# Attention on one core: the products with the values in two portions of 256 queries, other step costs in the plan, and later due times for the sums' transfers

## The chip, the core and the metric

The kernel runs on one core of a Trainium2 chip. The core has a TensorE (PE in the profile; PEld are its weight loads), a VectorE (DVE), a ScalarE (ACT), a GpSimd (POOL), a SyncE that only issues transfers (SP), and 16 DMA engines. The metric is the device time of one execution in microseconds (us); the figure for a kernel is the median of several executions.

## What is computed

Two kinds of layer alternate, twice: multi-head attention and a state-space convolution (S4D), each with a layer norm ahead and a residual sum behind. 2048 positions, 640 channels, 32 heads of 20 channels.

```python
def _A_ref(x, wqkv, wo):                     # attention
    qkv = (x @ wqkv).reshape(B, S, 3, H, Dh) ...
    scores = jnp.einsum("bhqd,bhkd->bhqk", q, k) * (Dh ** -0.5)
    p = _softmax(scores, axis=-1)
    o = jnp.einsum("bhqk,bhkd->bhqd", p, v)
    return o.transpose(0, 2, 1, 3).reshape(B, S, D) @ wo

def _B_ref(u, log_A_real, A_imag, C_real, C_imag, log_dt, D_skip):   # S4D
    P = jnp.exp((A * dt[:, None])[:, :, None] * pos[None, None, :])
    K = 2.0 * jnp.einsum("dn,dnl->dl", C, P).real    # convolution kernel, from the parameters alone
    y = irfft(rfft(u_t, 2 * L) * rfft(K, 2 * L)) ...
    return y + u * D_skip

x = x + _A_ref(_layernorm(x), A_wqkv, A_wo)
x = x + _B_ref(_layernorm(x), ...)
x = x + _A_ref(_layernorm(x), A_wqkv, A_wo)
x = x + _B_ref(_layernorm(x), ...)
```

## The kernel before, in words

**Stages.** Attention 1, output projection, S4D 1, attention 2, output projection, S4D 2. In attention 1 the S4D convolution kernel `K` is also made (`kgen`), since it depends on parameters alone; its second user, S4D 2, finds it stored. The change touches the two attention stages.

**One attention stage** is a loop over 8 groups `g` of four heads, 4 blocks `qb` of 512 queries and 16 blocks `kt` of 128 keys: 32 blocks (`g`, `qb`) of 16 steps `kt`. One step `kt` has two **waves** `j`, one for each pair of heads. A wave is: eight matmuls of the scores (L775, into the PSUM tile `S`), then one exponential on ACT (L778, `pt<-S`, 128x1024). There are 1024 waves in a stage; this text numbers them from 0 in each stage, so block (`g`, `qb`) begins at wave 128g + 32qb. Of `S` there are two buffers: the scores of wave n+2 wait for the exponential of wave n. Behind the second wave of a step come the products with the values (L792, `values`): eight float32 matmuls of 64 rows by 32 columns by 512 queries, into the two accumulators `pa`. The trace shows each float32 matmul as two records.

**What fills PE between the scores.** `jobs` yields steps of the projections for the later heads: `qk` steps of eight fp16 matmuls (L560, 15 steps for 512 queries of one 128-column block, four blocks `b` of 128 columns in all; their norms L488 close a block) and portions of the values of a group pair (`vq`, L524: 15 matmuls of 128x160 for each of 16 key tiles). In attention 1 there are also the contractions of `kgen` (L314, `contract`: two steps of 16 float32 matmuls each). `slot` puts one such step between two groups of scores if it fits by the plan.

**The plan.** The program is written out once, in Python; `Plan` holds three clocks (`pe`, `act`, `dve`) that are moved on by a cost in us for each step (0.22 for the scores, 0.865 for the values, 0.215 for a `qk` step, 0.43 for a contraction step, 0.63 for a portion of `vq`, 0.92 for an exponential). The order of PE's matmuls is fixed by it (`chain`), and so is the order of DVE's work and of the transfers on the queues of POOL and SP (`Ordered`). ACT's instructions and POOL's arithmetic are not tied: the scheduler places them. `AHEAD` is a table (wave, us of jobs done): contractions are taken only when the jobs are ahead of it. `need(...)` forces the jobs that a coming group depends on: block `b` of the projections must be complete, with norms, at `kt` = 10 of the last block ahead of the group that reads it (waves 116, 372, 500 and 756).

**The end of a block.** Behind its last values DVE adds the two accumulators (`oc<-pa`, twice). Then, at due times behind that (in us of the plan): `sums` (0.2) writes the rows of the denominators to memory (`dn<-oc`), `load` (5.0) reads them back in another shape (`dr<-dn`), `invert` (10.0) takes the reciprocal on DVE, `back` (11.0) writes it (`dn<-dr`), `spread` (15.5) reads it to all rows (`db<-dn`). At the end of the next block `scale` multiplies (`oc<-oc,db`) and `store` writes the result (`ot<-oc`). All these transfers are on POOL's queue, which also carries `kgen`'s loads of 576 KB (`kpw<-wd`) and stores (`kd<-ko`), and the bounds for the softmax (`qm<-mr`).

**The end of the stage.** When `kgen` is done and all heads are projected, `end_jobs` loads the output weights and splits them on POOL (`woh`, `wol`); `out_split` loads the first slices of the attention's result (`otl<-ot`) and splits them on ACT (`oh<-otl`) ahead of the output projection.

Of the kernel before, what the change touches and what calls it, by code (L numbers as in the profile page):

```python
# [29 lines left out]
NA, NB = 32, 64  # L30
LV = [1.0, 2.0, 4.0, 8.0, 16.0, 32.0, 64.0, 128.0, 256.0, 512.0, 1024.0, 1536.0]
PB = 7
AHEAD = ((0, 0.0), (96, 22.0), (352, 47.0), (478, 72.0), (724, 125.0))
WS = 256.0
LG = 2
BOUND = 30.0
# [45 lines left out]
def mha_s4d_kernel(ctx, tc, x_in, wqkv, wo, lar, aim, cr, ci, ldt, dsk,  # L82
# [96 lines left out]
    def kgen():  # L179
# [124 lines left out]
        def contract(r, bs, sub, ko, a, b):  # L304

            ps = pst("M", [P, 512], F32, tag=f"m{r}", name=f"m{r}")[:, :DC // 4 * NB].rearrange("p (c b) -> p c b", b=NB)
            for c8 in range(DC // 4):
                if c8:
                    yield plan.pe + 0.7, 0.43, True, ()
                plan.on_pe(0.43)  # L310
                for n in range(4):
                    for j in range(4):
                        ch, dd = DC * (sub % 2) + 4 * c8 + j, 4 * c8 + j
                        chain(te.matmul(ps[32 * j:32 * j + 32, c8, :], a[n // 2][:, ch, :], b[n][:, dd, :],  # L314
                                        start=(n == 0), stop=(n == 3), tile_position=(0, 32 * j)))
# [75 lines left out]
    def attention(x, stats):  # L391
# [121 lines left out]
        def values_of(i, q, ps, w, n):  # L513

            sl = slice(i * P, i * P + P)
            k = 0
            if n == QW:
                plan.on_pe(0.63)
            for ct in range(NCT):
                for a_, m in ((xh, w[0]), (xh, w[1]), (xl, w[0])):  # L520
                    if k == 8 and n == QW:
                        yield 0.0, 0.63, True, ()
                        plan.on_pe(0.63)
                    chain(te.matmul(ps[:, :n], a_[:, ct, sl], m[:, ct, :], start=(k == 0), stop=(k == 14)))  # L524
# [12 lines left out]
        def jobs():  # L537
# [40 lines left out]
            def vq(q):  # L578
                make = stage(2 * D + q * QW, QW, "v")
                yield plan.pe + 5.0, 0.0, False, ()  # L580
                w = make()
                t0 = plan.dve
                for i in range(NI):
                    yield t0, 0.63, False, (i % 2,)
# [38 lines left out]
        def slot(until=None):  # L623
# [4 lines left out]
            if pend and part[0] is None and not begun and (head[0] is None or spent[0] >= ahead(len(ends) - 2)):  # L628
# [1 line left out]
                r = free.index(min(free))  # L630
                t = max(t + 0.15, free[r])
                if t <= plan.pe or until is None and head[0] is None:
                    part[:] = f(r, *args), (t, 0.43, True, ())
                    pend.pop(0)
            step = part[1] if part[0] else head[0]
            if step is None:
# [144 lines left out]
            ends.append(plan.act)  # L781
            return pt

        def values(qb, g, kt, pts, pa):

            V = Vt[g // 2 % 3]
            plan.on_pe(0.865)
            for r in range(2):
                rows = slice(64 * r, 64 * r + 64)
                for j in range(4):  # L790
                    h = 4 * (g % 2) + j
                    chain(te.matmul(pa[r][32 * j:32 * j + 32, :], V[rows, kt, VP * h:VP * h + 32],  # L792
                                    pts[j // 2][rows, 512 * (j % 2):512 * (j % 2) + 512],
                                    start=(kt == 0), stop=(kt == NI - 1), tile_position=(64 * r, 32 * j)))
            if kt == NI - 1:
# [37 lines left out]
                def store():  # L833
# [1 line left out]
                        h = 4 * g + j  # L835
                        ge.dma_start(ot[h * DH:(h + 1) * DH, 512 * qb:512 * qb + 512], oc[32 * j:32 * j + DH, :])
                later.extend((plan.dve + n, f) for n, f in (
                    (0.2, sums), (5.0, load), (10.0, invert), (11.0, back), (15.5, spread)))
                later.sort(key=lambda e: e[0])
                scaled.append(scale)  # L840

# [22 lines left out]

        def fill(j):

            if ready:
                t = max(ready[0][0] + 0.15, 0.0 if ready[0][3] else sums_[0])
                if t <= plan.pe + 0.1 or j and len(ready) > 2:
                    plan.on_pe(0.0, t)  # L870
                    values(*ready.pop(0)[1:])
            while slot(plan.act - 0.5):
                pass
            drain_later()
            weave()
# [4 lines left out]
        for g in range(H // 4):  # L880
            need((0, 1, 1, 2, 3, 3, 4, 4)[g], ("v", g // 2))
            for qb in range(4):
# [9 lines left out]
                for kt in range(NI):  # L892
                    kc, pts = P * (kt % 8), []
                    for j in range(2):
                        pts.append(scores(kop[j][kt // 8], kc, qop[j][qb % 2]))
                        if j:
                            ready.append((plan.act, qb, g, kt, pts, pa))
                        fill(j)
                    if kt == 2:
                        for j in range(2):  # L900
# [519 lines left out]
```

## Time and profile before

| what | us |
|---|---|
| median of 3 runs | 2776.24 (2775.16 to 2778.0) |
| the profiled execution | 2777.71 |
| its span in the trace | 2775.8 |
| attention 1, first to last exponential | 111.8 to 1146.2 |
| attention 2, first to last exponential | 1564.0 to 2545.4 |
| busy: PE / ACT / DVE / POOL | 2544.2 / 2352.1 / 1469.0 / 821.2 |
| mean granted clock of TensorE | 0.987 |

A row of the timeline is: start in us from the span's start, time in us, engine, line, operation, out<-in, shape, xcount, and in brackets the engine's idle time just before and what ended it. Rows of one operation that follow each other are merged. A busy PE is not a PE at its peak: the end of a matmul is modelled and includes the time that it takes to run through the array, so the distance from one group's start to the next group's start is the better measure of what PE can do. L74 is the helper that records DVE's work and the transfers; such rows are told apart by their tiles.

### The profile page before, as it was taken

The numbers are of one execution on the slowest core, as the hardware profiler recorded it, in microseconds if no ns is written. First come the engines' busy times: TensorE is split into PE (matmuls) and PEld (weight loads), VectorE is DVE, ScalarE is ACT, GpSimd is POOL, SyncE is SP. The second block draws the span as 40 slices with busy tenths as digits, with TensorE's granted clock in tenths as the row PEclk, the third lists the DMA queues.
The fourth block names the chain that finished last, engine by engine and source line by source line (L and its number), as shares of the span: only waits on it lengthen the run. The fifth ranks groups of instructions, "written<-read, shape, count | busy, mean of one in ns | idle before, by whom it ended". The sixth has DMA issues, their size and how long they took to land.

```text
span 2775.8 us, 117573 instructions
## 1 busy us (share of the span) xinstructions
PE 2544.2 (92%) x51968; PEld 1436.6 (52%) x51968; DVE 1469.0 (53%) x3292; ACT 2352.1 (85%) x2781; POOL 821.2 (30%) x1232
## 2 busy tenths in 40 slices
PE   7898989999999997899999998999999888878998
PEld 3453544444444442587796544544444333335988
DVE  8645778978887870366777333332222100002865
ACT  8797989999999998645665698999999999997464
POOL 1112222323223324300573022222322422222376
PEclk9999999999999999999999999999999999999999
DMA  6512232323222223354543112111211211112365
GB/s 230 162 43 68 54 77 52 85 59 78 56 68 55 57 84 96 100 202 179 198 150 92 34 49 66 54 52 51 55 50 38 69 27 38 39 40 71 106 194 159
DMA packets 179128, 238.65 MB, mean 86 GB/s; under 512 B 36144, under 2 KB 124208, under 8 KB 176816
## 3 DMA queue, kind: packets, MB, share of 16 engines
q1 hardware_dynamic: 143168, 184.44, 20.6%
q0 software_dynamic: 35440, 46.58, 7.8%
q8 instruction: 410, 6.72, 1.0%
q14 instruction: 110, 0.90, 0.1%
HBM read 154.87 MB, written 76.03 MB: 83 GB/s over the span
## 4 chain that ended last, share of the span: by engine, by line
ACT 46%; PE 28%; issue 11%; DVE 7%; DMA 6%; POOL 1%; SPq 0%; ACTq 0%; DVEq 0%; POOLq 0%
ACT pt L778 46%; PE pa L792 4%; PE S L775 3%; PE psv L1148 3%; PE po L1054 3%; PE psy L1158 2%; PE psx L1136 2%; PE psx L1113 2%; PE po L1048 1%; DMA kop<-ks 1%; PE m L314 1%; PE pv L524 1%; PE pst L1123 1%; PE m L560 1%; PE pq L681 1%
## 5 line engine op out<-in xcount | busy, mean ns | idle before, releaser
L778 ACT ACTIVATE pt<-S 128x1024 f32<-128x1024 f32 x2048 | 1930.9, 1041 | 71.8 <-PE S L775 57.2
L792 PE MATMUL pa<-pt,V 64*32 64x512 f32 x16384 | 1099.6, 594 | 0.6 <-DVE oc L74 0.6
L775 PE MATMUL S<-qop,kop 61*32 61x512 f16 x16384 | 869.4, 383 | 160.6 <-ACT pt L778 138.0
L775 PEld LDWEIGHTS <-kop 61*32 61x32 f16 x16384 | 369.9, 90 | 830.7 <-issue 726.1
L74 POOL DMA_DIRECT2D dn<-oc x256 | 125.2, 496 | 835.6 <-DVE oc L74 768.2
L792 PEld LDWEIGHTS pa<-pt,V 64*32 64x32 f32 x16384 | 308.9, 107 | 69.4 <-issue 8.3
L74 DVE COPY oc<-pa 128x512 f32<-128x512 f32 x64 | 44.2, 691 | 414.8 <-PE pa L792 414.7
L74 DVE TENSOR_SCALAR qc<-m 128x512 f32<-128x512 f32 x64 | 44.1, 689 | 289.2 <-PE m L560 289.2
L74 POOL DMA_DIRECT2D db<-dn x256 | 129.3, 511 | 139.7 <-DMA dn<-dr 137.0
L74 DVE TENSOR_TENSOR kb<-ktab 128x512 f32<-128x512 f32 x240 | 155.3, 684 | 1.5 <-PE m L314 1.5
L560 PE MATMUL m<-xh,wh 64*32 64x512 f16 x2560 | 139.1, 380 | 3.0 <-DVE qc L74 3.0
L560 PE MATMUL m<-xh,wl 64*32 64x512 f16 x2560 | 138.3, 378 | 0.7 <-issue 0.7
L560 PE MATMUL m<-xl,wh 64*32 64x512 f16 x2560 | 138.4, 378 | 0.0
L74 POOL DMA_DIRECT2D ot<-oc x256 | 130.7, 517 | 8.9 <-DVE oc L74 6.0
L314 PEld LDWEIGHTS m<-kb,ka 128*32 128x32 f32 x5120 | 79.8, 110 | 101.6 <-issue 64.5
L560 PEld LDWEIGHTS <-wh 64*32 64x32 f16 x5120 | 87.7, 94 | 75.4 <-issue 37.6
L1141 POOL TENSOR_TENSOR t<-t,kb 128x512 f32<-128x512 f32 x80 | 102.1, 1276 | 70.3 <-DVE t L74 69.4
L1125 ACT COPY xt<-pst 128x1024 f16<-128x1024 f16 x80 | 81.6, 1023 | 46.7 <-PE pst L1123 46.5
L314 PE MATMUL m<-kb,ka 128*32 128x64 f32 x5120 | 105.8, 224 | 11.4 <-DVE qc L74 11.4
L74 POOL DMA_DIRECT2D dn<-dr x64 | 35.7, 557 | 234.1 <-DVE dr L74 229.8
L1142 POOL TENSOR_TENSOR t<-t,t 128x512 f32<-128x512 f32 x78 | 99.3, 1273 | 7.3 <-DVE t L74 1.3
L970 POOL TENSOR_TENSOR ul<-u,uh 128x640 f16<-128x640 f32 x30 | 46.5, 1566 | 177.7 <-ACT uh L969 177.7
(273 smaller groups left out, 3770.4 us busy)
## 6 DMA issues: line engine op xcount, KB each, us to landing
ka<-kha SPq DMA_DIRECT2D x80, 256.0 KB
kb<-khb SPq DMA_DIRECT2D x80, 256.0 KB
db<-dn POOLq DMA_DIRECT2D x256, 64.0 KB, 2.8
kpw<-wd POOLq DMA_DIRECT2D x20, 576.0 KB, 7.7
qop<-qs SPq DMA_DIRECT2D x256, 40.0 KB
kop<-ks SPq DMA_DIRECT2D x128, 80.0 KB
ot<-oc POOLq DMA_DIRECT2D x256, 40.0 KB, 2.6
otl<-ot SPq DMA_DIRECT2D x32, 320.0 KB
```

The lines of the kernel that those rows point to most:

```text
L74: made = f(out, *a, **k)
L314: chain(te.matmul(ps[32 * j:32 * j + 32, c8, :], a[n // 2][:, ch, :], b[n][:, dd, :], start=(n == 0), stop=(n == 3), tile_position=(0, 32 ...
L560: chain(te.matmul(ps[r][32 * t:32 * t + 32, :], a_[rows, ct, 32 * t:32 * t + 32], m[rows, ct, sl], start=(k == 0), stop=(k == 14), tile_po ...
L775: chain(te.matmul(S[32 * t:32 * t + 32, 512 * r:512 * r + 512], kt_[rows, kc + 32 * t:kc + 32 * t + 32], qt[rows, :], start=True, stop=Tru ...
L778: se.activation(pt, S, AF.Exp, scale=SCALE)
L792: chain(te.matmul(pa[r][32 * j:32 * j + 32, :], V[rows, kt, VP * h:VP * h + 32], pts[j // 2][rows, 512 * (j % 2):512 * (j % 2) + 512], sta ...
L1054: te.matmul(pos[hf], oh[:, ct, :], m[:, ct, 320 * hf:320 * hf + 320], start=False, stop=(ct == NCT - 1 and m is wol))
L1113: te.matmul(ps[:, r, i, :], e1[:, e, s, r, :], m[:, s, bs], start=(n == 0), stop=(n == 2))
L1125: se.copy(xt, pt.rearrange("p k g c -> p k (g c)"))
L1141: ge.tensor_mul(t2, t2, kb)
L1142: (ge if g0 else ve).tensor_add(t1, t1, t2)
L1148: te.matmul(pv[:, g].rearrange("p r i c -> p (r i c)"), t1[:, g * P:g * P + P], fa, start=True, stop=True)
```

## The change

The products with the values are cut in two portions of 256 queries (`half`), each planned at 0.433. A portion is queued by itself, and `fill` puts it between two groups of scores only if it ends 0.5 before the exponential does, or if more than five portions are waiting. A contraction step is counted at 0.56 where it was 0.43. A portion of `vq` ends every five matmuls (0.4 each) where it ended at the eighth (0.63 each). `AHEAD` asks for less of the jobs at most waves. The due times of `load`, `invert`, `back` and `spread` move from 5.0, 10.0, 11.0 and 15.5 to 6.0, 14.0, 14.5 and 20.0.

```diff
-AHEAD = ((0, 0.0), (96, 22.0), (352, 47.0), (478, 72.0), (724, 125.0))
+AHEAD = ((0, 0.0), (84, 20.0), (340, 44.0), (466, 68.0), (730, 122.0))
...
-                    yield plan.pe + 0.7, 0.43, True, ()
-                plan.on_pe(0.43)
+                    yield plan.pe + 0.7, 0.56, True, ()
+                plan.on_pe(0.56)
...
-                    if k == 8 and n == QW:
-                        yield 0.0, 0.63, True, ()
-                        plan.on_pe(0.63)
+                    if k % 5 == 0 and k and n == QW:
+                        yield 0.0, 0.4, True, ()
+                        plan.on_pe(0.4)
...
-        def values(qb, g, kt, pts, pa):
+        def values(half, qb, g, kt, pts, pa):
...
-            plan.on_pe(0.865)
+            plan.on_pe(0.433)
...
-                    h = 4 * (g % 2) + j
-                    chain(te.matmul(pa[r][32 * j:32 * j + 32, :], V[rows, kt, VP * h:VP * h + 32],
-                                    pts[j // 2][rows, 512 * (j % 2):512 * (j % 2) + 512],
-                                    start=(kt == 0), stop=(kt == NI - 1), tile_position=(64 * r, 32 * j)))
+                    h, c0 = 4 * (g % 2) + j, 256 * half
+                    chain(te.matmul(pa[r][32 * j:32 * j + 32, c0:c0 + 256], V[rows, kt, VP * h:VP * h + 32],
+                                    pts[j // 2][rows, 512 * (j % 2) + c0:512 * (j % 2) + c0 + 256],
+                                    start=(kt == half == 0), stop=(half == 1 and kt == NI - 1), tile_position=(64 * r, 32 * j)))
...
-                    (0.2, sums), (5.0, load), (10.0, invert), (11.0, back), (15.5, spread)))
+                    (0.2, sums), (6.0, load), (14.0, invert), (14.5, back), (20.0, spread)))
...
-            if ready:
-                t = max(ready[0][0] + 0.15, 0.0 if ready[0][3] else sums_[0])
-                if t <= plan.pe + 0.1 or j and len(ready) > 2:
-                    plan.on_pe(0.0, t)
-                    values(*ready.pop(0)[1:])
+            def half(late):
+                if not ready:
+                    return False
+                t = max(ready[0][0] + 0.15, 0.0 if ready[0][4] else sums_[0])
+                if not late and (t > plan.pe + 0.1 or plan.pe + 0.433 > plan.act - 0.5):
+                    return False
+                plan.on_pe(0.0, t)
+                values(*ready.pop(0)[1:])
+                return True
+            while len(ready) > 5:
+                half(True)
+            while len(ready) > 2 and half(False):
+                pass
             while slot(plan.act - 0.5):
                 pass
+            while half(False):
+                pass
...
-                            ready.append((plan.act, qb, g, kt, pts, pa))
+                            ready.extend((plan.act, n, qb, g, kt, pts, pa) for n in range(2))
```

Three places where the order moves, as the built programs have it.

PE in attention 1 ahead of the scores of wave 758 (tiles: `S` scores, `pa` the values' accumulators, `m` the PSUM tile of a projection or contraction). Before:

```order
L775 LDWEIGHTS kop_104
L775 MATMUL S<-qop_108,kop_104 32x512
L792 MATMUL pa_21160<-pt,V_94 32x512 x4
L792 MATMUL pa_21161<-pt,V_94 32x512 x4
L775 LDWEIGHTS kop_102
L775 MATMUL S<-qop_106,kop_102 32x512
```

And of the change, at the same wave:

```order
L775 LDWEIGHTS kop_104
L775 MATMUL S<-qop_108,kop_104 32x512
L792 MATMUL pa_23682<-pt,V_94 32x256 x4
L792 MATMUL pa_23683<-pt,V_94 32x256 x4
L792 MATMUL pa_23682<-pt,V_94 32x256 x4
L792 MATMUL pa_23683<-pt,V_94 32x256 x4
L314 MATMUL m_24258<-kb_24032,ka_23867 32x64 x4
L314 MATMUL m_24258<-kb_24033,ka_23867 32x64 x4
L314 MATMUL m_24258<-kb_24034,ka_23868 32x64 x4
L314 MATMUL m_24258<-kb_24035,ka_23868 32x64 x4
L524 LDWEIGHTS xh
L524 MATMUL m_24336<-vh,xh 128x160
```

Between the same two groups of scores there now stand both portions of the values, a contraction step, the 15 matmuls of a whole key tile of `vq` (the first of them is the last row shown) and then the norms L488 of the last projected block, which stood ahead of wave 743 before.

POOL's queue around the end of block 6 (it ends at wave 224), before:

```order
L74 DMA dn<-oc 16x1x32 x4
L74 DMA ot<-oc 20x512 x4
L74 DMA kpw_166<-wd 128x36x32
L74 DMA dr<-dn 128x16
L74 DMA dn<-dr 128x16
L74 DMA db<-dn 32x512 x4
```

And of the change:

```order
L74 DMA dn<-oc 16x1x32 x4
L74 DMA ot<-oc 20x512 x4
L74 DMA dr<-dn 128x16
L74 DMA dn<-dr 128x16
L74 DMA db<-dn 32x512 x4
L74 DMA kd<-ko 128x8x64
L74 DMA kpw_165<-wd 128x36x32
```

The load of the sums (`dr<-dn`) stood behind a load of `kgen` and now stands ahead of it.

ACT near the end of attention 1, before:

```order
L530 ACTIVATE V_94<-pv 128x8x20
L778 ACT_TABLE_LOAD
L778 ACTIVATE pt<-S 128x1024 x970
L956 CAST oh<-otl 128x640 x2
L778 ACTIVATE pt<-S 128x1024 x54
L956 CAST oh<-otl 128x640
```

And of the change:

```order
L778 ACTIVATE pt<-S 128x1024 x980
L966 CAST oh<-otl 128x640
L778 ACTIVATE pt<-S 128x1024 x8
L966 CAST oh<-otl 128x640
L778 ACTIVATE pt<-S 128x1024 x36
L966 CAST oh<-otl 128x640
```

The first two splits of the attention's result moved from behind 970 exponentials to behind 980 and 988. In attention 2 they stay behind 970. The last contraction stands ahead of wave 961 where it stood ahead of wave 911, and `end_jobs` moves from wave 928 to wave 992.

More of the change, by code (lines that the diff above doesn't have):

```diff
@@ L517, in values_of @@
             if n == QW:
-                plan.on_pe(0.63)
+                plan.on_pe(0.4)
             for ct in range(NCT):
                 for a_, m in ((xh, w[0]), (xh, w[1]), (xl, w[0])):
-                    if k == 8 and n == QW:
-                        yield 0.0, 0.63, True, ()
-                        plan.on_pe(0.63)
+                    if k % 5 == 0 and k and n == QW:
+                        yield 0.0, 0.4, True, ()
+                        plan.on_pe(0.4)
                     chain(te.matmul(ps[:, :n], a_[:, ct, sl], m[:, ct, :], start=(k == 0), stop=(k == 14)))
@@ L583, in vq @@
                 for i in range(NI):
-                    yield t0, 0.63, False, (i % 2,)
+                    yield t0, 0.4, False, (i % 2,)
                     yield from values_of(i, q, pst("M", [P, 512], F32, tag=f"m{i % 2}", name=f"m{i % 2}"), w, QW)
@@ L632, in slot @@
                 if t <= plan.pe or until is None and head[0] is None:
-                    part[:] = f(r, *args), (t, 0.43, True, ())
+                    part[:] = f(r, *args), (t, 0.56, True, ())
                     pend.pop(0)
@@ L790, in values @@
                 for j in range(4):
-                    h = 4 * (g % 2) + j
-                    chain(te.matmul(pa[r][32 * j:32 * j + 32, :], V[rows, kt, VP * h:VP * h + 32],
-                                    pts[j // 2][rows, 512 * (j % 2):512 * (j % 2) + 512],
-                                    start=(kt == 0), stop=(kt == NI - 1), tile_position=(64 * r, 32 * j)))
-            if kt == NI - 1:
+                    h, c0 = 4 * (g % 2) + j, 256 * half
+                    chain(te.matmul(pa[r][32 * j:32 * j + 32, c0:c0 + 256], V[rows, kt, VP * h:VP * h + 32],
+                                    pts[j // 2][rows, 512 * (j % 2) + c0:512 * (j % 2) + c0 + 256],
+                                    start=(kt == half == 0), stop=(half == 1 and kt == NI - 1), tile_position=(64 * r, 32 * j)))
+            if half and kt == NI - 1:
                 blk = 4 * g + qb
```

## The prediction

> **What bounds the kernel now.** I read the page's list of groups first, then the exponentials in windows, then the timeline of PE and of DVE where ACT waits. The change touches the two attention stages alone; ahead of them and behind them the order of PE is the same but for a few rows.
>
> ```profile
> L778 ACT ACTIVATE pt<-S 128x1024 f32<-128x1024 f32 x2048 | 1930.9, 1041 | 71.8 <-PE S L775 57.2
> ...
> 111.80:1146.20 1034.40, 973.57 (x1024) 0.98 0.27 66
> 1564.00:2545.40 981.40, 957.28 (x1024) 0.99 0.17 47
> 2200.00:2450.00 250.00, 249.94 (x273) 1.00 0.13 35
> ```
>
> The last three rows are the exponentials alone: window, its length, busy time, count. From 2200 on PE has nothing but scores and values, and ACT never waits: 249.94 / 273 = 0.9155 us for a wave, 1.83 for a step of two. At that rate 1024 waves take 937.5, so attention 1 lies 96.9 us and attention 2 43.9 us above ACT's own time. This is all that the change can win. The page shows 71.8 of it as idle time of ACT; the rest is exponentials that start just late enough not to overlap the one ahead.
>
> The first part of it is PE itself, where a step holds too much:
>
> ```profile
> 700.91 0.41 PE L775 MATMUL S<-qop,kop 61*32 61x512 f16 x8
> 701.13 1.04 PE L792 MATMUL pa<-pt,V 64*32 64x512 f32 x16
> 702.00 0.40 PE L775 MATMUL S<-qop,kop 61*32 61x512 f16 x8
> 702.32 0.65 PE L314 MATMUL m<-kb,ka 128*32 128x64 f32 x32
> 702.91 0.41 PE L775 MATMUL S<-qop,kop 61*32 61x512 f16 x8
> ```
>
> From start to start: scores 0.22, values 0.87, scores up to the contraction 0.32 (0.10 of it is the entry into the other form), contraction 0.59. The step is 2.00, or 0.17 over ACT's 1.83, though the plan counts 0.22 + 0.865 + 0.22 + 0.43 = 1.74. Two more forms:
>
> ```profile
> 263.98 0.41 PE L775 MATMUL S<-qop,kop 61*32 61x512 f16 x8
> 264.20 0.41 PE L560 MATMUL m<-xl,wh 64*32 64x512 f16 x8
> ...
> 264.85 0.41 PE L775 MATMUL S<-qop,kop 61*32 61x512 f16 x8
> ```
>
> ```profile
> 704.00 0.40 PE L775 MATMUL S<-qop,kop 61*32 61x512 f16 x8
> 704.33 0.24 PE L524 MATMUL m<-vh,xh 128*128 128x160 f16 x1
> ...
> 704.82 0.23 PE L524 MATMUL m<-vl,xh 128*128 128x160 f16 x1
> 704.99 0.41 PE L775 MATMUL S<-qop,kop 61*32 61x512 f16 x8
> ```
>
> A wave with three `qk` steps (each 0.22; the order has three between these two rows of scores) takes 0.87 (with the values' wave 1.96, 0.13 over). One with eight matmuls of `vq` takes 0.99 (2.08, 0.25 over): 0.22, eight times 0.07, and 0.21 for the entry; seven of them make 0.18 over, ten would make 0.39.
>
> The second part is waits of DVE that reach ACT:
>
> ```profile
> 261.38 1.87 POOL L74 DMA_DIRECT2D kpw<-wd  x1
> ...
> 263.25 0.56 POOL L74 DMA_DIRECT2D dr<-dn  x1
> ...
> 267.66 0.51 PE L775 MATMUL S<-qop,kop 61*32 61x512 f16 x8
> 268.95 0.17 DVE L74 TENSOR_SCALAR dr<-dr 128x16 f32<-128x16 f32 x1 [4.57 <-DMA dr<-dn]
> ...
> 271.81 0.84 PE L314 MATMUL m<-kb,ka 128*32 128x64 f32 x32 [3.65 <-DVE qc L74]
> ...
> 273.35 1.02 ACT L778 ACTIVATE pt<-S 128x1024 f32<-128x1024 f32 x1 [4.03 <-PE S L775]
> ```
>
> DVE stands 4.57 at `invert`, since the sums were read back behind a load of `kgen`; the emptying of a projection (`qc`) is queued behind it, PE's contraction waits 3.65 for that PSUM tile, the scores stand behind the contraction, and ACT waits 4.03. The same at the end of block 6:
>
> ```profile
> 367.80 0.18 DVE L74 TENSOR_SCALAR dr<-dr 128x16 f32<-128x16 f32 x1 [4.03 <-DMA dr<-dn]
> ...
> 372.43 1.02 ACT L778 ACTIVATE pt<-S 128x1024 f32<-128x1024 f32 x1 [5.87 <-PE S L775]
> ...
> 374.56 2.00 ACT L778 ACTIVATE pt<-S 128x1024 f32<-128x1024 f32 x2 [1.11 <-PE S L775]
> ```
>
> **The change part by part**, against the profiled execution's 2777.7.
>
> *Portions and plan.* By the order, the 160 contraction steps still share a step with both portions of the values (135 waves hold a contraction alone, 24 one with a portion): 2.00 as before, no gain. What changes is the rest. Attention 1 before: 88 waves with three `qk` steps, 10 with four, 16 with eight and 16 with seven matmuls of `vq`: 88 x 0.13 + 10 x 0.35 + 16 x 0.25 + 16 x 0.18 = 21.8 us over. Of the change: 75, 5 and 9 with ten matmuls: 75 x 0.13 + 5 x 0.35 + 9 x 0.39 = 15.0. The others became two waves of one portion and one `qk` step, 2 x (0.22 + 0.435 + 0.22) = 1.75, which fits. Attention 2: 91, 8, 32, 32 give 28.4; 65, 6 and 28 give 21.5. The gain is 6.8 + 6.9 = 13.7 if no slack is carried from one step to the next, and nothing if all of it is. I take half, **-7**.
>
> *Price of a portion.* No row shows 256 float32 columns. From below it is half of 0.87, since sixteen matmuls of twice the columns pass in that; from above by the line through two rows: groups of 64 columns pass in 0.59 / 8 = 0.073, groups of 512 in 0.435, which leaves 0.021 for each group whatever its length, and 2 x 0.021 = 0.042 more for each step. I take half of 0.87: a `qk` group with fp16 passes 512 columns in 0.22, so that a float32 group at 0.435 is just twice that and leaves nothing fixed. The upper end is a rival below.
>
> *More entries.* `vq` now stands in 38 waves instead of 33, and in 69 instead of 65: 9 x 0.21 = 1.9, half of it where PE has slack: **+1**. The Trainium skill (TensorEngine Tiling, Key Properties) says that a change of the tiling mode drains the array; the 0.10 and 0.21 above agree. By that rule alone, three portions for each of 16 + 32 key tiles instead of two would cost 48 x 0.21 = 10; the order joins most of them, so I hold to the count.
>
> *Due times.* `invert` comes 3 later behind `load` than before (8 for 5), and in the two blocks shown the load no longer stands behind `kpw`. The waits were 4.57 and 4.03; both go: 4.03 + 5.87 + 1.11 = **-11**. What is then late next is the PSUM tile itself, by less than 1.
>
> *The end of attention 1.*
>
> ```profile
> 1027.59 2.79 SPq L74 DMA_DIRECT2D wot<-in_wo  x5
> ...
> 1050.41 3.05 POOL L939 TENSOR_TENSOR wol<-wot,woh 128x640 fp32r<-128x640 f32 x2
> ...
> 1084.55 2.04 POOL L74 DMA_DIRECT2D ot<-oc  x4 [2.42 <-DVE oc L74]
> ...
> 1089.65 0.95 SPq L74 DMA_DIRECT2D otl<-ot  x2
> ...
> 1093.16 1.58 ACT L956 CAST oh<-otl 128x640 fp32r<-128x640 f32 x2 [7.43 <-DMA otl<-ot]
> ...
> 1099.51 1.94 ACT L778 ACTIVATE pt<-S 128x1024 f32<-128x1024 f32 x2 [1.11 <-PE S L775]
> ```
>
> ACT's queue holds the two splits behind 970 exponentials, and their data comes 7.43 late. Behind 980 the first has 9.2 us more. It costs 0 to 8.5; the second, behind 988, follows three loads of `x` on SP's queue and may wait a little. I take **-8**. `end_jobs` comes 64 waves later, at wave 992; from the load of `wo` to the last of POOL's work on it are 25.9 us (1027.59 to 1053.46), and the 32 waves that are left take 29.3, so it hides still, with little to spare.
>
> *Forced jobs.* The order has 96 `qk` matmuls ahead of wave 118 instead of 16: ten steps of 0.22, less a portion that moved away: **+2**. And the norms of block 4 now come at wave 758, ten waves before the first scores that need them. Before, this distance stood only at wave 118:
>
> ```profile
> 231.79 0.40 PE L488 MATMUL m<-sq,sel 128*32 128x512 bf16 x3 [1.60 <-DVE qc L74]
> ...
> 233.37 9.75 ACT L778 ACTIVATE pt<-S 128x1024 f32<-128x1024 f32 x10 [3.08 <-PE S L775]
> ...
> 236.81 2.07 POOL L74 DMA_DIRECT2D qm<-mr  x4 [1.02 <-DVE flag L74]
> ...
> 245.62 0.25 SPq L74 DMA_DIRECT2D qop<-qm  x1
> ...
> 248.72 0.58 PE L775 MATMUL S<-qop,kop 61*32 61x512 f16 x1 [4.58 <-DMA qop<-qm]
> 250.47 1.03 ACT L778 ACTIVATE pt<-S 128x1024 f32<-128x1024 f32 x1 [5.77 <-PE S L775]
> ...
> 252.60 1.03 ACT L778 ACTIVATE pt<-S 128x1024 f32<-128x1024 f32 x1 [1.11 <-PE S L775]
> ...
> 895.06 7.88 ACT L778 ACTIVATE pt<-S 128x1024 f32<-128x1024 f32 x8 [0.46 <-PE S L775]
> ```
>
> From norms to bounds (`qm`), from there through SP's queue to `qop`: 17 us, of which ten waves hide ten. ACT lost 3.08 + 5.77 + 1.11 = 10. At wave 768 it lost 0.46 (the last row). So **+9.5**, between 0 and 10.
>
> The sum: -7 + 1 - 11 - 8 + 2 + 9.5 = -13.5, which is 2764.2. The profiled execution lies 1.5 above the median of the runs, so **2763**.
>
> **The rivals.**
>
> *The chain at wave 758 is hidden* (SP issues the loads of `kop` and `qop` ahead of it, and only two of four heads need block 4). Against it stands the row at 248.72, where the same two heads were late. 9.5 less: 2753.
>
> *DVE waits elsewhere*: `spread` comes 4.5 later, POOL's queue holds `kgen`'s loads at other places, and a wait for `db` at `scale` would block DVE as the one for `dr` did. For it speaks that blocks 14 and 26 again have `kpw` ahead of the load. The 11 are not won: 2774.
>
> *A fixed price for each group*: 0.042 for each of the 249 + 99 steps that are over 1.83 is 14.6: 2778. This is also the way of a rule in the Trainium skill (TensorEngine Tiling, Instruction Overhead): each matmul carries an overhead of some 60 cycles, so a dimension that is already small is not to be cut.
>
> *Slower: PE's instructions come no faster.*
>
> ```profile
> 400.00:450.00 50.00, 49.45 (x1476) 23.73 (x1465) 47.60 (x112) 48.80 (x52) 18.05 (x28) 1.00 0.33 77
> ```
>
> The highest rate that any 50 us show is 2941 matmuls and weight loads, 59 in a us. With portions, waves 64 to 95 of attention 1 hold 2 x (256 + 512 + 288) = 2112 in 29.3, 72 in a us. If the rate stops at 65, such a block takes 32.5; with half of these 3.2 us lost in each of 43 blocks with jobs, 69 us: 2832. It decides from 59 upward. Against it: 264.85 - 263.98 holds 64 records in 0.87, 74 in a us, if only for that long.
>
> **How the numbers follow.** Forecast 0.54, chain hidden 0.12, DVE elsewhere 0.14, fixed price 0.10, rate 0.10. The first four lie between 2753 and 2778; with the full 13.7 for the portions on the low side and a few us of new waits on the high one the range is 2747 to 2781. A measurement can tell 0.2% (5.6 us) from no change. Faster by more: 0.54 + 0.12 + 0.02 = 0.68; within: most of 0.14 and 0.10, 0.18; slower: 0.10 and the upper ends, 0.14.
>
> **What would show it.** Right: a step with a contraction still 2.00; a portion at 0.22 to 0.23 for each of its two groups; no wait of DVE for `dr` over 2 us ahead of wave 900 and none of ACT there; no wait of ACT at the splits in attention 1; a wait of 5 to 8 at wave 768. Wrong: portions dearer than 0.45, ACT waiting where the second split stands, or a wait of DVE for `db`.

## The result

| | us |
|---|---|
| the kernel of the change, median of 4 runs | 2871.34 (2868.99 to 2873.87) |
| the kernel before, median of 4 runs | 2775.70 (2772.21 to 2778.00) |
| ratio, 95% interval | 1.0346 (1.0328 to 1.0364) |
| span of the profiled execution, after / before | 2872.0 / 2775.8 |
| attention 1, first to last exponential's start, after / before | 1111.1 / 1033.3 (+77.8) |
| attention 2, the same | 992.2 / 980.4 (+11.8) |

The change makes the kernel 3.5% slower; the prediction was 2763, 0.5% faster. Of the rest, 1.6 lie between the stages and 5.0 ahead of attention 1, where executions differ by as much (the first exponential starts between 111.5 and 116.8 in the runs of this text). Two of the runs below, the halves back to back and the changed kernel with late splits, had one execution each at a granted clock of 0.75 and 0.70 (3277 and 3449 us), which their times leave out.

The exponentials alone, in windows of the changed kernel (window, its length, ACT busy and count, granted clock, DMA share, GB/s): the two stages, and a stretch with nothing but scores and values.

```profile
116.80:1229.00 1112.20, 977.16 (x1024) 0.98 0.25 62
1648.40:2641.60 993.20, 955.30 (x1024) 0.99 0.17 47
2300.00:2550.00 250.00, 249.95 (x273) 1.00 0.15 36
```

In the quiet stretch ACT still never waits. The loss lies where PE has jobs. On the page of the changed kernel (busy time and instructions, queue 8, and the costliest groups with their idle time and what ended most of it):

```profile
PE 2608.2 (91%) x68352; PEld 1755.5 (61%) x68352; DVE 1469.0 (51%) x3292; ACT 2353.0 (82%) x2781; POOL 821.3 (29%) x1232
...
q8 instruction: 538, 8.81, 1.3%
...
L778 ACT ACTIVATE pt<-S 128x1024 f32<-128x1024 f32 x2048 | 1932.5, 1038 | 149.2 <-PE S L775 132.0
L792 PE MATMUL pa<-pt,V 64*32 64x256 f32 x32768 | 1254.0, 379 | 19.6 <-issue 16.0
...
L792 PEld LDWEIGHTS pa<-pt,V 64*32 64x32 f32 x32768 | 672.9, 106 | 234.5 <-issue 51.0
```

Four rows of the page of before belong beside it:

```profile
PE 2544.2 (92%) x51968; PEld 1436.6 (52%) x51968; DVE 1469.0 (53%) x3292; ACT 2352.1 (85%) x2781; POOL 821.2 (30%) x1232
...
q8 instruction: 410, 6.72, 1.0%
...
L792 PE MATMUL pa<-pt,V 64*32 64x512 f32 x16384 | 1099.6, 594 | 0.6 <-DVE oc L74 0.6
...
L792 PEld LDWEIGHTS pa<-pt,V 64*32 64x32 f32 x16384 | 308.9, 107 | 69.4 <-issue 8.3
```

ACT's idle time behind the scores has doubled (71.8 to 149.2). The new kind of idle time is "issue" on the products themselves: time in which PE waits for nothing that the profile shows (16.0 and 51.0 us on matmuls and weight loads, none and 8.3 before). Queue 8 carries instructions: 128 packets more for 32,768 more matmuls and weight loads, which is 256 for each packet.

The distance from the start of one wave's scores to the start of the next wave's, by what stands between them in attention 1, worked out from the trace (median in us, mean, count):

```
                                        before                after
the whole product                  1.080  1.123 (507)    1.085  1.196 (295)
a portion and one qk step              -                 0.876  0.963 (132)
a portion alone                        -                 0.692  0.758  (82)
a contraction                      0.914  1.048 (156)    0.927  1.054 (115)
three qk steps                     0.867  0.935  (87)    0.869  1.044  (60)
```

The fastest portion alone took 0.653 with its scores (0.22), so a portion is 0.43: half a product, as forecast. Contractions and `qk` steps have kept their medians as well. Where a median stays and a mean grows, nothing has become dearer; something stops now and then. One such stop, in the timeline of the changed kernel:

```profile
1020.77 0.41 PE L775 MATMUL S<-qop,kop 61*32 61x512 f16 x8 [0.54 <-ACT pt L778]
...
1020.99 1.06 PE L792 MATMUL pa<-pt,V 64*32 64x256 f32 x24
...
1022.72 0.14 PEld L792 LDWEIGHTS pa<-pt,V 64*32 64x32 f32 x5 [1.15 <-issue]
1022.72 0.42 PE L792 MATMUL pa<-pt,V 64*32 64x256 f32 x4 [0.67 <-issue]
...
1023.70 2.86 ACT L778 ACTIVATE pt<-S 128x1024 f32<-128x1024 f32 x3 [1.14 <-PE S L775]
```

PE breaks off in the middle of a product, behind 24 of its 32 matmuls, and goes on 1.05 us later. Its operands were there: the 16 matmuls of the first portion had read the same `pt` and `V`. What it lacked, by the count below, were instructions. The packet that was under way on queue 8 ran from 1019.78 to 1021.39, and PE went on 1.33 after it had landed. The longest distance of the first block from one exponential to the next, 3.7 us at wave 5, is of the same kind: a packet from 122.57 to 124.14, and PE starts nothing for 2.86 until 125.72.

That can be counted. Packet k holds the 256 instructions that follow a fixed place in PE's order. Of the packets of the changed kernel between 130 and 500 us, not one had its first instruction start sooner than 1.2 us after it had landed, and half had it start within 1.5: PE was standing there. In the kernel before half of them started later than 2.6. A border counts as a stop below if PE was idle for over 0.15 us and went on 1.15 to 1.7 us after the landing; "turn" is the time from the end of one packet to the start of the next.

```
                                turn, us (5%, 50%)   packets   borders with a stop   us of stops
before, attention 1                 2.50   3.58         201               4               3.0
after, attention 1                  2.41   2.67         265             115              71.4
after, attention 2                  2.43   2.98         226              22               9.3
```

A packet takes 1.1 us on average, and in attention 1 of the changed kernel the next one starts 2.4 (5%) to 2.7 us (median) behind its end, 2.24 at the least. So one packet is under way at a time, and a cycle of 3.5 to 3.8 us for 256 instructions is 73 to 67 in a us. The 2.7 have two parts: 1.5 from the landing to the packet's first instruction, and 1.1 from there to the start of the next packet (medians). The Trainium skill (Runtime: NRT & Kernel Launch, Instruction fetch mechanics) says that instructions are refilled in blocks of 16 KiB, 256 each, and that crossing a block's border is mostly hidden. The trace agrees on the block (each packet is 16,384 bytes); that it is hidden holds for the kernel before (3.0 us of stops in attention 1) and not for this one (71.4).

One wait of attention 2 is of another kind. At wave 512 the changed kernel needs 6.3 us from one exponential to the next, where the kernel before needs 0.9:

```profile
2152.61 0.36 SPq L74 DMA_DIRECT2D qop<-qm  x1
...
2154.21 0.21 SPq L74 DMA_DIRECT2D qop<-qm  x1
...
2156.57 0.58 PE L775 MATMUL S<-qop,kop 61*32 61x512 f16 x1 [4.13 <-DMA qop<-qm]
...
2158.22 1.02 ACT L778 ACTIVATE pt<-S 128x1024 f32<-128x1024 f32 x1 [5.29 <-PE S L775]
```

The four runs below that keep the plan with portions have 4.8 to 5.4 us there, merged or not; the seven without it, the halves back to back among them, have an ordinary wave. So it comes with the order and not with the number of instructions. Why the transfer comes late was not tested.

### The profile page after: what moved, and what is told of

Its sections match the earlier page's. It is cut to its first block, busy times and chain, and to the rows that moved or that the text cites. A ratio compares the mean times of both kernels' runs of the same rounds, so it can differ in the third digit from the quotient of the medians.

```text
span 2872.0 us, 150345 instructions
## 1 busy us (share of the span) xinstructions
PE 2608.2 (91%) x68352; PEld 1755.5 (61%) x68352; DVE 1469.0 (51%) x3292; ACT 2353.0 (82%) x2781; POOL 821.3 (29%) x1232
## 4 chain that ended last, share of the span: by engine, by line
PE 59%; ACT 24%; issue 7%; DVE 5%; DMA 4%; POOL 1%; SPq 1%; ACTq 0%; DVEq 0%; POOLq 0%
ACT pt L778 22%; PE pa L792 19%; PE S L775 11%; PE m L560 6%; PE m L314 3%; PE po L1064 3%; PE psv L1158 3%; PE psy L1168 2%; PE m L524 2%; PE psx L1146 2%; PE psx L1123 2%; PE pv L524 1%; PE po L1058 1%; PE pq L681 1%; PE pst L1133 1%
## 5 line engine op out<-in xcount | busy, mean ns | idle before, releaser
L778 ACT ACTIVATE pt<-S 128x1024 f32<-128x1024 f32 x2048 | 1932.5, 1038 | 149.2 <-PE S L775 132.0
L792 PE MATMUL pa<-pt,V 64*32 64x256 f32 x32768 | 1254.0, 379 | 19.6 <-issue 16.0
L775 PE MATMUL S<-qop,kop 61*32 61x512 f16 x16384 | 957.7, 384 | 168.6 <-ACT pt L778 132.3
L792 PEld LDWEIGHTS pa<-pt,V 64*32 64x32 f32 x32768 | 672.9, 106 | 234.5 <-issue 51.0
L560 PE MATMUL m<-xl,wh 64*32 64x512 f16 x2560 | 169.0, 380 | 4.2 <-issue 3.9
L560 PE MATMUL m<-xh,wh 64*32 64x512 f16 x2560 | 166.5, 381 | 6.0 <-issue 3.5
L560 PE MATMUL m<-xh,wl 64*32 64x512 f16 x2560 | 170.2, 380 | 0.2
L560 PEld LDWEIGHTS <-wh 64*32 64x32 f16 x5120 | 113.5, 94 | 63.1 <-issue 24.4
L524 PEld LDWEIGHTS <-xh 128*128 128x128 f16 x800 | 69.7, 98 | 57.9 <-issue 37.2
```

The lines of the kernel that those rows point to most:

```text
L560: chain(te.matmul(ps[r][32 * t:32 * t + 32, :], a_[rows, ct, 32 * t:32 * t + 32], m[rows, ct, sl], start=(k == 0), stop=(k == 14), tile_po ...
L775: chain(te.matmul(S[32 * t:32 * t + 32, 512 * r:512 * r + 512], kt_[rows, kc + 32 * t:kc + 32 * t + 32], qt[rows, :], start=True, stop=Tru ...
L778: se.activation(pt, S, AF.Exp, scale=SCALE)
L792: chain(te.matmul(pa[r][32 * j:32 * j + 32, c0:c0 + 256], V[rows, kt, VP * h:VP * h + 32], pts[j // 2][rows, 512 * (j % 2) + c0:512 * (j % ...
```

## The experiments

**Theory 1**: PE is short of instructions. **Theory 2**: the new order is worse. **Theory 3**: a portion costs more than half a product. Each run was made beside the kernel before on the same chip; its median there was 2777.13 for the run with three products, the two runs with due times and the run with space of its own, 2774.60 for the last three runs of this section, and 2774.34 for the other four.

**Two portions that stand next to each other, written as one product** (everything else as in the change):

```diff
+            if half == 0 and not now:
+                held.append((half, qb, g, kt, pts, pa))
+                return
+            c0, n = (0, 512) if held else (256 * half, 256)
+            held.clear()
...
-                    chain(te.matmul(pa[r][32 * j:32 * j + 32, c0:c0 + 256], ...
+                    chain(te.matmul(pa[r][32 * j:32 * j + 32, c0:c0 + n], ...
```

> The changed kernel, but where both portions of a step come directly after one another on PE they are written as one product of 512 queries; every decision of the plan is the same, so the order of all other work is that of the changed kernel. 672 of 1024 steps of both stages together become whole again, PE's instructions fall by about 21,500. Theory 1 (PE is short of instructions: it is supplied in packets of 256, and no faster than one packet in 3.4 to 3.9 us, so that the 115 packet borders of attention 1 at which PE stood 71 us in the changed kernel are the loss): most of these stops go, 2795 to 2815 us. Theory 2 (the order is worse: gates, contraction counted longer, jobs forced together): no gain, 2860 to 2872. Theory 3 (a portion costs PE more than half of a product): 2840 to 2872, since most steps that were over in the changed kernel hold a single portion and stay.

Measured: 2803.10, ratio 1.0102 (1.0082 to 1.0122). 68 of the 95.6 us are gone with the instructions alone; the plan decided the same. In attention 1, 28 borders of 223 still have a stop, 21.3 us in all.

**The kernel before, each product in two halves back to back:**

```diff
+            n = 256
+            for c0 in range(0, 512, n):
...
-                    chain(te.matmul(pa[r][32 * j:32 * j + 32, :], ...
+                        chain(te.matmul(pa[r][32 * j:32 * j + 32, c0:c0 + n], ...
```

> The kernel before, its plan and order untouched, but each product is issued as two of 256 queries, one right behind the other. PE's columns are the same, its instructions are as many as in the changed kernel. Theory 1 (supply of instructions): blocks of attention 1 hold 2000 to 2360 matmuls and weight loads, 8 to 9.2 packets of 256 at 3.6 us, 29 to 33 us for 29.3 of ACT, with local bursts above that: 2820 to 2865 us. Theory 2 (order): 2776, within 5. Theory 3 (a portion is dearer): a step of whole and contraction grows from 2.00 by the same amount everywhere, and the quiet part of attention 2 as well if PE's slack there (0.3 us a step) is passed.

Measured: 2855.17 (the median of three executions), ratio 1.0304 (1.0276 to 1.0333). No plan, no order and no due time differs from before; the halves alone cost 81 us. A wave with its scores and the whole product still passes in 1.084 at the median (1.080 before), so theory 3 is out; attention 1 has 119 stops, 71.9 us.

**Four products of 128 queries, in the quiet part alone** (blocks 20 to 31 of attention 2; n is 128 there, otherwise as above):

> The kernel before, but in the last 12 blocks of attention 2, where PE has nothing but scores and values and ACT never waits, each product is issued as four of 128 queries. Theory 1: a block holds 2564 matmuls and weight loads, 10 packets at 3.5 us (1.07 of transfer and 2.45 from one packet's end to the next one's start): 35 us for 29.4, over 11 blocks 60 to 70 us more, 2835 to 2845; PE stops at every packet border. Theory 2: 2776, as no order changes. Theory 3, as a price of 0.021 for each group of eight: 0.13 a step, inside the slack: 2776; as weight loads that do not hide (64 at 24 ns in a step): 0.15 over 1.83 a step, 2800.

Measured: 2864.28, ratio 1.0323 (1.0305 to 1.0342). Here no job, no plan and no order takes part, and a block takes 36 to 39 us for 29.5. Busy times in 250 us of that part (window, its length, PE, PEld, DVE, ACT and POOL with their counts, granted clock, DMA share, GB/s):

```profile
2230.00:2480.00 250.00, 182.16 (x8432) 132.48 (x8433) 14.45 (x30) 201.42 (x212) 44.62 (x88) 0.99 0.11 28
```

The same of the kernel before, in the window of the prediction:

```profile
2200.00:2450.00 250.00, 203.04 (x4344) 84.15 (x4329) 19.80 (x42) 249.94 (x273) 68.76 (x131) 1.00 0.13 35
```

The products of the run on its page:

```profile
L794 PE MATMUL pa<-pt,V 64*32 64x512 f32 (+1 forms) x25600 | 1150.3, 440 | 57.1 <-issue 55.4
```

8432 matmuls and 8433 weight loads in 250 us are 67.5 in a us, and that is all that comes; the kernel before had 35 there. PE is idle for a fourth of the time and ACT for a fifth. The fastest wave with scores and four products passed in 1.088, as with one product: neither the columns nor the loads of weights are the limit. (Less 0.22 for the scores, 0.87 hold 64 weight loads and their matmuls, 0.014 for each pair; no run shows the 24 ns for a weight load that the expectation took for theory 3.) The stage has 106 stops, 104.8 us. The forecast was 19 us too low at its upper end: it took 3.5 us for a packet, and the median cycle was 3.76.

**Three products there: 256, 128 and 128 queries:**

> The kernel before, but in the last 12 blocks of attention 2 each product is issued as three: 256, 128 and 128 queries. A block holds 2052 matmuls and weight loads, 8.0 packets. Theory 1 (supply): at the 3.77 us a packet of the run with four of 128 that is 30.2 us for 29.5, at the 3.5 us of the least disturbed packets 28.1, so the block stands at the edge: 29.4 to 30.6, all in all 0 to 14 us, 2774 to 2790, with stops at a part of the packet borders. Theory 3 (each 128-query portion has a price of its own): half of what the run with four lost, as half of the extra portions are there: 2815 to 2825.

Measured: 2782.36, ratio 1.0017 (1.0008 to 1.0027), blocks of 29.6 to 29.8 where nothing else disturbs. The same window of this run:

```profile
2230.00:2480.00 250.00, 211.53 (x8595) 140.84 (x8590) 19.28 (x40) 247.68 (x269) 56.84 (x112) 1.00 0.14 35
```

69 instructions in a us can be had, with a few stops in the whole stage (2 us in all); at the 87 that four products would need (2564 in a block of 29.5) the same place is starved. The edge lies between, and the 67.5 that came there put it near 70. Two of the three extra portions cost 5 us, all three cost 90: it is a threshold, not a price.

**The rest of the change without the portions:**

```diff
+AHEAD = ((0, 0.0), (84, 20.0), (340, 44.0), (466, 68.0), (730, 122.0))
+                    yield plan.pe + 0.7, 0.56, True, ()
+                    if k % 5 == 0 and k and n == QW:
+                    (0.2, sums), (6.0, load), (14.0, invert), (14.5, back), (20.0, spread)))
```

> The kernel before with the rest of the change and without the portions: contraction counted 0.56, the new advance table, projections of the values in steps of five, the new due times; values stay whole and as the old rule places them. Theory 1: no loss, 2760 to 2785 (the prediction's terms for the due times, -11, are in it). Theory 2: a good part of the 95 us, 2810 or more.

Measured: 2788.07, ratio 1.0043 (1.0025 to 1.0061): 14 us slower, three over the expectation of theory 1. So the order costs something too, about a seventh of the loss. The norms of block 4 come at wave 758, and ACT waits at wave 768, in the timeline of this run:

```profile
886.25 0.40 PE L488 MATMUL m<-sq,sel 128*32 128x512 bf16 x4
...
890.26 2.12 POOL L74 DMA_DIRECT2D qm<-mr  x4 [1.02 <-DVE k2m L74]
...
901.64 0.58 PE L775 MATMUL S<-qop,kop 61*32 61x512 f16 x1 [5.34 <-DMA qop<-qs]
...
905.51 1.02 ACT L778 ACTIVATE pt<-S 128x1024 f32<-128x1024 f32 x1 [8.05 <-PE S L775]
...
907.65 1.02 ACT L778 ACTIVATE pt<-S 128x1024 f32<-128x1024 f32 x1 [1.11 <-PE S L775]
```

Distances of 9.8 us at wave 384 and 5.8 at wave 453, where the kernel before had 1.7 and none, are of this run's table and count as well.

**The due times alone**, and **the due times with steps of five for `vq`** (the third and fourth line of the diff above):

> The kernel before with the new due times alone. The prediction's term: the waits of DVE for the sums at blocks 3 and 6 go, 11 us, 2763 to 2767. Rival: load and spread, now later, meet other loads on POOL's queue, and DVE waits elsewhere: 2774 or more. (If the 13.7 us that the plan without portions lost came from the due times, this shows it: 2785 or more.)

> The kernel before with the new due times and with the projections of the values in steps of five matmuls, the advance table and the contraction's count as before. If the table and the count made the loss of the plan without portions (waits at waves 384, 453 and 768 of attention 1): 2760 to 2768. If the steps of five did (more entries into the other form, 0.21 each): 2775 to 2788.

Measured: 2773.19, ratio 0.9987 (0.9976 to 0.9998), and 2772.00, ratio 0.9984 (0.9975 to 0.9993). Both gains are small and neither meets its expectation: the first lies above 2763 to 2767, the second between its two cases. The steps of five cost nothing, so the loss of the run before is the table and the contraction's count. `invert` no longer waits at the end of blocks 3 and 6 (first row below, for block 3; at 368.22 for block 6). But at wave 256 the scores now wait for `qop`, and ACT loses there 2.4 and another 1.2 more than before; `spread`'s four transfers go out just ahead of the last part of that load, which may be the reason but was not tested. In the timeline of the first of the two:

```profile
270.98 0.17 DVE L74 TENSOR_SCALAR dr<-dr 128x16 f32<-128x16 f32 x1
...
374.00 2.02 POOL L74 DMA_DIRECT2D db<-dn  x4 [4.48 <-DMA dn<-dr]
...
378.60 0.21 SPq L74 DMA_DIRECT2D qop<-qm  x1
...
382.20 0.37 PE L775 MATMUL S<-qop,kop 61*32 61x512 f16 x1 [3.58 <-DMA qop<-qm]
...
383.87 1.02 ACT L778 ACTIVATE pt<-S 128x1024 f32<-128x1024 f32 x1 [4.54 <-PE S L775]
```

**The end of attention 1.** In the changed kernel ACT stands 15 us at the first split:

```profile
1152.71 3.46 SPq L74 DMA_DIRECT2D wot<-in_wo  x5
...
1157.87 1.40 POOL L948 CAST woh<-wot 128x640 fp32r<-128x640 f32 x2
...
1178.66 1.53 POOL L949 TENSOR_TENSOR wol<-wot,woh 128x640 fp32r<-128x640 f32 x1
1180.22 0.38 SPq L74 DMA_DIRECT2D otl<-ot  x1
...
1183.65 0.72 ACT L966 CAST oh<-otl 128x640 fp32r<-128x640 f32 x1 [14.98 <-DMA otl<-ot]
```

The load of `otl` is issued 0.03 us after POOL's last work on `wot`, whose space it takes. First try, space of its own:

```diff
+        w2 = c.enter_context(tc.tile_pool(name="wo2", bufs=2, side="right"))
         with tc.tile_pool(name="wos", bufs=NCT, side="right") as ws:
```

> The changed kernel, but the buffers that the first output slices are loaded into (otl) have space of their own instead of that of the staged projection weights (wot), so that their load does not wait until POOL has made the last of those into wol. Theory: the 16.7 us that ACT stood at the first split, and most of the 4.0 at the second, are this wait; 6 to 10 us stay, as in the kernel before, for the data themselves: 2855 to 2865. Rival: the load is late because the sums of block 28 are late (the due times): no gain, 2868 to 2872.

Measured: 2872.65, ratio 1.0347 (1.0331 to 1.0363): no gain. In the profiled execution (2861.32) the load goes out at 1157.46, during POOL's work, and ACT stands 8.44 instead of 14.98; but the split has also moved ahead, behind 970 exponentials instead of 980, and the other three executions took 2871.4 to 2873.9. The wait for the space is shown, its worth in the whole is not.

Second try, the split itself held back on ACT until the newest exponential:

```diff
-            se.activation(pt, S, AF.Exp, scale=SCALE)
+            newest[0] = se.activation(pt, S, AF.Exp, scale=SCALE).ins
...
-            se.copy(oh, cur)
+            tie(se.copy(oh, cur), newest[0] if s < 2 else None)
```

> The changed kernel with the first two splits (oh<-otl) held on ACT until the exponential that is newest where the program calls them: behind 1014 and 1024 exponentials of a stage, not 980 and 988. Theory: ACT's wait of 16.7 and 4.0 us in attention 1 and of 6 us in attention 2 was nothing but a split standing in ACT's queue ahead of its data; it goes, 18 to 26 us: 2846 to 2854. Rival: the time between the stages grows by what the stages lose, since the projection behind them waits for the splits instead: 2865 to 2872.

Measured: 2854.90 (the median of three executions), ratio 1.0281 (1.0258 to 1.0305). 16 us are gone, 2 fewer than the least expected; the two splits of attention 1 no longer wait.

**A version that beats both**: the kernel before with the new due times, `vq` in steps of five, and the late splits.

> The kernel before with the new due times, steps of five for the projections of the values, and the late splits of the run above: a try at a version better than both. The waits at wave 969 (6.7 and 6.6 us in the run without late splits, of which 0.9 is an exponential's own time, and 1.2 behind them) go from both stages: 9 to 13 us less than that run's 2772: 2759 to 2764. Rival as above: 2770 or more.

Measured: 2758.97, ratio 0.9944 (0.9931 to 0.9958). Its two stages:

```profile
113.30:1130.50 1017.20, 971.32 (x1025) 0.99 0.27 67
1548.60:2524.60 976.00, 956.88 (x1024) 0.99 0.17 47
```

**Portions with everything else mended**: merged where they are neighbours, the table and the count of before, late splits.

> The changed kernel with portions written as one product wherever they are next to one another, the contraction counted as before with the advance table of before, and late splits: whether portions pay at all where the supply of instructions allows them. If the loss of the merged run (29 us over the kernel before) is the table and the count (13 to 16) and the wait at the splits (8 in attention 1, 6 in attention 2), this comes to 2768 to 2780. If the split steps still starve PE at packet borders (21 us of stops in the merged run), 2780 to 2795.

Measured: 2784.65, ratio 1.0034 (1.0022 to 1.0045), the second of the two cases: 41 borders of 227 in attention 1 have a stop, 26.3 us. Beside them stand 7.3 us from one exponential to the next at wave 640 of attention 1 and 5.4 at wave 512 of attention 2, neither of which the run above has. Portions do not pay here even so, and against the run above they cost 26 us.

## Why the prediction was wrong

**The step that failed is the rival "PE's instructions come no faster".** It was there, with the right mechanism, but it was given 0.10, and the sum of the forecast has no term for it; the runs showed some 80 us of stops in its place. It was put aside by one row: 64 records in 0.87 us, 74 in a us. A burst of 64 says nothing of the supply. In the trace a packet starts when about 230 of the instructions that have landed are left (the median in the kernel before). With the 256 under way that is not quite two packets, up to 7 us of work at 74 in a us (an estimate), and a burst shorter than that can pass at PE's own speed. The rate that counts is the one that lasts longer than the store. Counted by the rows of the prediction, it was at hand: a step with the whole product and three `qk` steps has 32 + 32 + 48 = 112 records in 1.96 us, 57 in a us, and one with a contraction 128 in 2.00, 64. With portions they have 144 and 160, or 73 and 80, where some 70 can be had.

Its size was off too. It was priced at 2832: a limit of 65, and half of 3.2 us in each of 43 blocks. The limit is better than that, near 70, but there is no halving: the shortage is one of single steps, which the average of a block (2000 to 2260 records in most blocks of attention 1, 68 to 77 in a us at ACT's 29.3) hides, and where PE has waited for something else, the store gives back two packets at most. The stops, 71.4 + 9.3 = 80.7 us, go nearly whole into the time: with the halves back to back, some 77 us more of them than before stand beside 81 us lost, and merging took 56 us of them away with 68 us.

**Portions and plan, -7.** The class times came out as forecast (0.876 for a portion with a `qk` step where 0.875 was worked out; a contraction with the whole product 1.085 + 0.927 = 2.01 for 2.00). The gain of 7 is not seen: in the steps that were made to fit, the mean lies 0.09 above the median, as stops would make it. That the stops take the whole gain is not shown.

**Price of a portion.** Right: 0.43. The rival of a fixed price for each group falls with it, and so does the rule of the Trainium skill (TensorEngine Tiling (Array Packing), Instruction Overhead) as the reason: groups of 128 queries passed as fast as groups of 512 until instructions ran out (1.088 and 1.080 for a wave), and no run here shows such an overhead.

**More entries, +1.** Not measurable: the two runs with the due times differ by 1.2 us, within their intervals, and the one with more entries is the faster.

**Due times, -11.** The mechanism was right, the size was not: alone they are worth 3.9 (2777.13 to 2773.19). The waits at blocks 3 and 6 went, and what came in their place is the rival "waits elsewhere", only that ahead of wave 900 it was PE that waited for `qop` and once DVE for `dr` (3.71 us at 881.85), not DVE for `db`. In the changed kernel one such wait for `dr` is left there, 4.68 us at 824.33, and ACT loses nothing by it.

**End of attention 1, -8.** Wrong in sign: 16.7 and 4.0 us from one exponential to the next at the two splits, against 10.0 before. The step that failed is "so it hides still, with little to spare": it set the 25.9 us of POOL's work against the 32 waves behind `end_jobs`, but in the trace the load of `wot` goes out at about wave 964 and the split stands at wave 980, 16 waves behind, and its own load waits for the space of `wot`. The run with late splits is 16 us faster, and 11 of them are in attention 1 (1111.1 to 1099.8 in the profiled executions).

**Forced jobs, +2 and +9.5.** Right, within 2 us: the distances at waves 768 and 769 of the changed kernel are 9.2 and 2.1 us, in the plan without portions 9.1 and 2.1, where the kernel before has 1.5 at 768 and an ordinary wave behind it. At wave 117 the changed kernel has 7.6 for 4.1. Not foreseen was that the new table and count, without the portions, also make waits at waves 384 and 453, and that the plan with portions makes one at wave 512 of attention 2.

Added up: 68 by the portions' instructions as far as merging takes them away, 14 by the rest of the plan, and at the splits of attention 1 some 11 us more than before (16.7 + 4.0 - 10.0), make 93 of the 95.6, if the parts add. They overlap, for the wait at wave 512 of attention 2 (5 us) would come on top, and the 29 us that the merged run still loses have to hold its 21 us of stops as well as the plan, the splits and that wait. This, and why the plan's table costs more in one block than another, was not taken apart further.

## What to carry to other kernels

Count PE's instructions for each us of the stage's bound, weight loads and the second record of a float32 matmul included: each of eight float32 matmuls here is four. In this kernel cutting a product was free as long as that stayed under some 70 over any stretch of more than about 7 us: two portions in the quiet part of the changed kernel (52 in a us) left ACT without a wait. Beyond it PE stops at the borders of its instruction packets, wherever in a product these fall, and the profile shows it only as "issue", as means that grow under medians that stay, and in the packets of queue 8. An instruction that a scheduler puts into the queue of the bounding engine ahead of its data costs the wait (16 us here): tie it behind the work that it may not hold up.

## What the runs showed of the hardware

- PE's instructions come in packets of 16,384 bytes, 256 instructions, on a queue of their own. A packet took 1.08 to 1.16 us on average in the attention stages of every run. In the changed kernel no first instruction started sooner than 1.2 us after its packet had landed, and the next packet started 2.4 to 2.7 us after the landing. That gave 67.5 instructions in a us where PE was starved throughout (four products of 128); 69 were had at a loss of 5 us over twelve blocks.
- The traces show no more than about two packets held for PE: in the kernel before a packet starts when 230 of the instructions that have landed are left (the median), and in the changed kernel 1.1 us behind the first instruction of the packet ahead of it (the median).
- Eight float32 products of 64 rows by 32 columns and the scores of a wave pass in 1.08 us whether they are cut into groups of 512 or 256 queries (the medians), and in 1.09 with groups of 128 where instructions are there (the fastest).
